# Attention and mixture of experts on one core: the last batch's first loads moved to the head of the second block

## The chip, the cores and the metric

The kernel runs on one core of a Trainium2 chip. The metric is device time in microseconds (us), the median of several executions of the whole program. The core has five engines with a queue of instructions each: TensorE (PE in the rows; PEld is its weight load), VectorE (DVE), ScalarE (ACT), GpSimd (POOL) and SyncE (SP), which issues most of the DMAs.

## The reference, cut to what matters

Kernel-feature attention over 4 batches, 8 heads, 576 positions and head size 64, with 128 features, and then a dense mixture of 4 experts over all 2304 rows, all in fp32:

```python
def phi(x):
    proj = np.einsum('bhsd,md->bhsm', x, omega)
    h = proj - np.sum(x * x, axis=-1, keepdims=True) / 2.0
    h = h - np.max(h, axis=-1, keepdims=True)
    return np.exp(h) / np.sqrt(m)
q_p, k_p = phi(q * scale), phi(k * scale)
kv = np.einsum('bhsm,bhsd->bhmd', k_p, v)
num = np.einsum('bhsm,bhmd->bhsd', q_p, kv)
den = np.einsum('bhsm,bhm->bhs', q_p, k_p.sum(2))[..., None] + 1e-06
x = (num / den)                       # to 2304 rows of 512
for e in range(4):
    out += p[:, e:e + 1] * (np.maximum(x @ w1[e], 0.0) @ w2[e])
```

## The kernel before, in words

The experts' work is cut into visits: one visit is half an expert's hidden units (4 tiles of 128, so 8 visits in all) against one block of rows. The first rows are done in plain visits beside the attention of batches 0 to 2. Then comes the second block, 768 rows, in 8 fast visits (`fast`, L892), and the third block, 1024 rows, in 8 deep ones. Every fp32 operand is split in two parts, a high and a low one (`split`, L562), and every product is three matmuls. A fast visit builds its hidden units from seven products (`product`, L926, `p1` to `p7`) of 6 matmuls for each of two groups. ScalarE's `keep` (L938) copies a product out of PSUM before the next product is added on top of it: the fourth product, `p6(0)`, waits for the copy of the first. After the products come six output tiles of 12 matmuls (`outputs`, L748), and each is added to its accumulator by `gather` (L765), on ScalarE in the first visit of the second block (L780) and on VectorE after that (L782).

Beside its own matmuls a fast visit makes the w1 operands of the next one (`sides`, L672): ScalarE copies the high parts `w1ah` and `w1sh` (L564), GpSimd subtracts for the low parts `w1al` and `w1sl` (L567), VectorE adds in between (`add`, L682). `keep_sides` (L663) writes these operands to DRAM for the third block: eight `kept` stores (L670) per visit. There are two buffers of each kind, so the next visit's `w1ah` cannot be written before this visit's has been stored. The w2 rows come through three `w2r` buffers (L549).

The attention of the last batch has four pairs of heads and is spread over the second block in ticks: `opening` (L375) has six for the first pair (load k; load q; load v and tails; square k; square q; lengths of k), and `later_ticks` (L466) twelve for each pair. A pair needs the projection of keys and of queries on TensorE (`k_ps`, `q_ps`, `t_ps`, L266, L277), maxima and a bias on VectorE (L282 to L293; `nbk`, `nbq` are the biases), exponentials on ScalarE (`kp`, `qp`, L299, L306), squares on GpSimd (L251) with lengths on VectorE (L255), then sums, transposes and quotients.

The order of all work is the order in which the program is written (a manual schedule): each engine and SP's DMA queue run their instructions in that order. `emit` (L1379) runs the visits, and each visit yields after its products and after each output tile; after a yield of 1 the loop takes ticks until their count has reached `done * per`. For the second block `per` is 54 ticks over 44.8 yields.

Of the kernel before, what the change touches and what calls it, by code (L numbers as in the profile page):

```python
# [14 lines left out]
def attention_moe(ctx, tc, kT, qT, kd, qd, kn, qn, vn, omT, probs, w1, w2, out):  # L15
# [11 lines left out]
    _, NP, D, _ = kT.shape  # L27
# [3 lines left out]
    E, FP, P, _ = w1.shape  # L31
# [34 lines left out]
    def bank(name):  # L66
        return psum.tile([P, 512], F32, tag="ps", name=name)
# [33 lines left out]
    NV = len(HALVES)  # L101
# [273 lines left out]
    def opening(p, both=False):  # L375

        p.load("k")
        yield
        p.load("q")
        yield  # L380
        p.load_v()
        p.load_tails()
        yield
        p.square("k")
        yield
        p.square("q")
        yield
        p.lengths("k")
        if both:
            p.lengths("q")  # L390
        yield
# [74 lines left out]
    def later_ticks(pairs):  # L466

        for p, then in zip(pairs, pairs[1:] + [None]):
            p.project("k")
            p.project_tails("k")  # L470
            p.maxima("k")
            p.maxima_tails("k")
            p.bias("k")
            yield
            p.exp_tails("k")
            p.exp("k", 0)
            p.lengths("q")
            yield
            p.exp("k", 1)
            yield  # L480
            p.project("q")
            p.project_tails("q")
            p.maxima("q")
            p.maxima_tails("q")
            p.bias("q")
            yield
            p.exp_tails("q")
            p.exp("q", 0)
            if then:
                then.load("k")  # L490
            yield
            p.exp("q", 1)
            if then:
                then.load("q")
            yield
            p.sum_keys()
            if then:
                then.load_v()
                then.square("k")
            yield  # L500
            p.turn(0)
            yield
            p.turn(1)
            if then:
                then.square("q")
            yield
            p.numerators(0)
            if then:
                then.lengths("k")
            yield  # L510
            p.invert(0)
            p.times(0)
            p.numerators(1)
            yield
            p.invert(1)
            p.times(1)
            yield
# [4 lines left out]
    BIG = {1: (START, 6 * P), 2: (START + 6 * P, 8 * P)}  # L522
# [5 lines left out]
    N0 = len(visits)  # L528
# [204 lines left out]
    def hidden(v, f, n, ps, heads):  # L733
        (a, r), c0 = W[v, "w1", f], visits[v][3]
        for hp in heads:
            w = slice(place(hp) * P, (place(hp) + 1) * P)
            hi, lo = (x[:, c0:c0 + n] for x in x_first[hp])
            nc.tensor.matmul(ps[:, :n], a[:, w], hi, start=(hp == 0), stop=False)  # L738
            nc.tensor.matmul(ps[:, :n], a[:, w], lo, start=False, stop=False)  # L739
            nc.tensor.matmul(ps[:, :n], r[:, w], hi, start=False, stop=(hp == NP - 1))  # L740

    def relu(ps, n):
        ha, hc = (held([P, n], x) for x in ("hh", "hl"))
        nc.scalar.activation(ha, ps[:, :n], AF.Relu)
        nc.vector.scalar_tensor_tensor(hc, ps[:, :n], 0.0, f32(ha), ALU.max, ALU.subtract)
        return ha, hc

    def outputs(v, hs, ps, t, cs):  # L748

        ts_ = slice(t * P, (t + 1) * P)  # L750
        for c in cs:
            (ha, hc), (wa, wc) = hs[c], W[v, "w2", c]
            nc.tensor.matmul(ps, ha[:, ts_], wa, start=(c == 0), stop=False)  # L753
            nc.tensor.matmul(ps, ha[:, ts_], wc, start=False, stop=False)  # L754
            nc.tensor.matmul(ps, hc[:, ts_], wa, start=False, stop=(c == FH - 1))  # L755
# [47 lines left out]
    def plain(v):  # L803
        n = visits[v][4]
        last = v == N0 - 1
        ready = sides(v + 1) if last else iter(())
        hs = []
        for f in range(FH):
            ps = bank("g1")
            hidden(v, f, n, ps, range(2))  # L810
            if n > 2 * P:
                yield 0.5
            hidden(v, f, n, ps, range(2, NP))
            hs.append(relu(ps, n))
            split_w()
            if f != 1:
                next(ready, None)
            if last and f:
                next(building, None)
            yield 0.5  # L820
        tiles = n // P
        for t in range(tiles):
            ps = bank("g2")
            outputs(v, hs, ps, t, range(2))
            if v == N0 - 2 and t in (0, 2):
                next(building)
            if last:
                next(building, None)
            yield 0.5
            outputs(v, hs, ps, t, range(2, FH))  # L830
            gather(v, ps, t)
            gathered(v, t)
            for _ in range(FH // tiles):
                split_w()
            next(ready, None)
            if last:
                next(building, None)
            yield 0.5
# [476 lines left out]
    def first_visit(g1):  # L1315
        hs = [relu(ps, 2 * P) for ps in g1[:2]]
        yield 0.5
        for ps in g1[2:]:
            split_w(lo=nc.vector)
            hs.append(relu(ps, 2 * P))  # L1320
            yield 0.5
        split_w(lo=nc.vector)
        split_w(lo=nc.vector)
        yield 0.5
        for t in range(2):
            ps = bank("g2")
            outputs(0, hs, ps, t, range(FH))
            gather(0, ps, t)
            gathered(0, t)
            split_w()  # L1330
            split_w(lo=nc.vector)
            yield 1
# [40 lines left out]
    def chain(*many):  # L1373
        for x in many:
            yield from x
# [3 lines left out]
    def emit():  # L1379
        pairs, g1 = begin()  # L1380
        later = [Halves(b, hp) for b in range(1, B) for hp in range(NP)]
        windows = {
            0: (first_rest(pairs, opening(later[0], both=True)), 15 / 11),
            3: (joint_ticks(later[:-NP]), 76 / 45.4),
            N0: (chain(opening(later[-NP]), later_ticks(later[-NP:])), 54 / (NV * (BIG[1][1] // P + 1) * 0.8)),
        }
        ticks, n, done, per = iter(()), 0, 0.0, 0
        for v in range(len(visits)):
            if v in windows:
                for _ in ticks:  # L1390
                    pass
                ticks, per = windows[v]
                n, done = 0, 0.0
            for share in first_visit(g1) if v == 0 else fast(v) if v >= N0 else plain(v):
                done += share
                while n < done * per:
                    next(ticks, None)
                    n += 1
        store(0)
# [61 lines left out]
```

## Time and profile before

| | us |
|---|---|
| median of 3 executions | 888.69 (887.83 to 889.95) |
| the profiled execution, its own time | 889.82 |
| its span, first to last instruction | 888.0 |
| second block (8 fast visits) in the span | about 284.5 to 570.7 |
| granted TensorE clock | 1.00 over the span |

The profile shows one execution. Times in its rows are us from the start of the span, durations in the by-line rows are named by their unit. A timeline row merges equal instructions that follow each other ("x4") and ends with the idle time before it and what ended it, where there was any.

### The profile page before, as it was taken

The page shows a single profiled execution, that of the slowest core. Times are in us where ns is not written, and L with a number is a line of the kernel's source. Part 1 is how long each engine was busy: PE and PEld are TensorE (multiplying, and loading weights), DVE is VectorE, ACT ScalarE, POOL GpSimd, SP SyncE. Part 2 cuts the span into 40 slices and gives each one's busy share as a digit, 9 for nine tenths or more (in the row PEclk, how much of TensorE's full clock was granted, in tenths as well). Part 3 has the DMA queues.
Part 4 walks back from the last instruction along what each step waited for, and adds up shares of the span by engine and source line. Part 5 has one row for each costly group of instructions (what it writes and reads, how often), then busy time and mean ns, then how long its engine had stood idle before and what let it go on. Part 6 is the DMA issues. An engine that isn't in the chain of part 4 may idle for free.

```text
span 888.0 us, 14766 instructions
## 1 busy us (share of the span) xinstructions
PE 878.8 (99%) x5484; PEld 789.4 (89%) x5484; DVE 590.9 (67%) x1025; ACT 470.2 (53%) x1039; POOL 563.7 (63%) x494
## 2 busy tenths in 40 slices
PE   9999999999999989999999999999999999999998
PEld 9988888989888888989888899899989898998988
DVE  5765566666677556576766756975858476675847
ACT  6554677776774555555554554544443434444442
POOL 6656465555644454443545346779898887979874
PEclk9999999999999999999999999999999999999999
DMA  7675345444521847536375354644152442415132
GB/s 183 164 223 158 110 161 176 128 137 139 183 72 48 297 123 262 198 131 236 88 262 169 116 213 160 235 152 154 60 178 75 149 155 86 155 60 179 46 121 95
DMA packets 64296, 134.01 MB, mean 151 GB/s; under 512 B 10368, under 2 KB 20800, under 8 KB 64224
## 3 DMA queue, kind: packets, MB, share of 16 engines
q1 hardware_dynamic: 54256, 102.95, 35.3%
q0 software_dynamic: 9360, 29.82, 10.4%
q8 instruction: 43, 0.70, 0.3%
q10 hardware_dynamic: 608, 0.30, 0.1%
q14 instruction: 29, 0.24, 0.1%
HBM read 98.96 MB, written 34.08 MB: 150 GB/s over the span
## 4 chain that ended last, share of the span: by engine, by line
PE 92%; DVE 3%; DMA 2%; issue 1%; POOL 1%; ACT 1%; SPq 0%; POOLq 0%; ACTq 0%
PE g L934 28%; PE g L1009 18%; PE g L753 8%; PE g L755 7%; PE g L754 7%; PE g L738 3%; PE g L739 3%; PE g L740 3%; PE kv L317 2%; PE q_ps L266 1%; PE k_ps L266 1%; PE qt_ps L328 1%; PE k_ps L147 1%; DMA kept<-w1ah 1%; PE q_ps L147 1%
## 5 line engine op out<-in xcount | busy, mean ns | idle before, releaser
L782 DVE SCALAR_TENSOR_TENSOR acc<-g,pr,acc 128x256 f32<-128x256 f32 (+1 forms) x278 | 139.2, 540 | 37.0 <-PE g L755 27.5
L567 POOL TENSOR_TENSOR w2l<-w2r,w2h 128x512 fp32r<-128x512 f32 x61 | 79.3, 1305 | 80.4 <-ACT w2h L564 68.2
L567 POOL TENSOR_TENSOR w1sl<-w1r,w1sh 128x512 fp32r<-128x512 f32 (+1 forms) x43 | 75.1, 1747 | 64.3 <-ACT w1sh L564 53.4
L753 PE MATMUL g<-w2h,hh 128*128 128x512 f32 x280 | 112.0, 400 | 1.8 <-DVE sum L946 1.6
L755 PE MATMUL g<-w2h,hl 128*128 128x512 f32 x280 | 109.7, 392 | 0.0
L754 PE MATMUL g<-w2l,hh 128*128 128x512 f32 x280 | 109.5, 391 | 0.0
L959 DVE SCALAR_TENSOR_TENSOR hl<-sum,hh 128x384 fp32r<-128x384 f32 (+1 forms) x64 | 48.3, 757 | 81.5 <-ACT hh L955 71.7
L946 DVE TENSOR_TENSOR sum<-g,sum 128x384 f32<-128x384 f32 (+1 forms) x96 | 59.3, 619 | 61.2 <-PE g L934 52.8
L934 PE MATMUL g<-xbh,w1sh 128*128 128x384 f32 (+1 forms) x256 | 93.1, 364 | 2.4 <-ACT sum L940 2.4
L934 PE MATMUL g<-xbl,w1sh 128*128 128x384 f32 (+1 forms) x256 | 92.9, 363 | 0.0
L934 PE MATMUL g<-xbh,w1sl 128*128 128x384 f32 (+1 forms) x256 | 92.6, 362 | 0.0
L940 ACT ACTIVATE sum<-g 128x384 f32<-128x384 f32 (+1 forms) x96 | 52.1, 543 | 69.2 <-PE g L934 68.3
L567 POOL TENSOR_TENSOR w1al<-w1r,w1ah 128x512 fp32r<-128x512 f32 (+1 forms) x45 | 51.4, 1157 | 52.2 <-ACT w1ah L564 35.4
L934 PE MATMUL g<-xbh,w1ah 128*128 128x384 f32 (+1 forms) x192 | 70.0, 365 | 0.0
L934 PE MATMUL g<-xbl,w1ah 128*128 128x384 f32 (+1 forms) x192 | 69.6, 362 | 0.0
L934 PE MATMUL g<-xbh,w1al 128*128 128x384 f32 (+1 forms) x192 | 69.5, 362 | 0.0
L753 PEld LDWEIGHTS g<-w2h,hh 128*128 128x128 f32 x280 | 52.6, 188 | 12.7 <-DVE sum L946 2.2
L755 PEld LDWEIGHTS g<-w2h,hl 128*128 128x128 f32 x280 | 52.5, 188 | 11.8 <-DVE hl L992 0.4
L754 PEld LDWEIGHTS g<-w2l,hh 128*128 128x128 f32 x280 | 52.6, 188 | 9.0
L955 ACT ACTIVATE hh<-sum 128x384 fp32r<-128x384 f32 (+1 forms) x64 | 35.0, 548 | 43.9 <-DVE sum L946 43.5
L934 PEld LDWEIGHTS g<-xbh,w1sh 128*128 128x128 f32 x256 | 48.1, 188 | 8.4 <-ACT sum L940 2.7
L934 PEld LDWEIGHTS g<-xbl,w1sh 128*128 128x128 f32 x256 | 48.1, 188 | 5.1
(214 smaller groups left out, 2475.3 us busy)
## 6 DMA issues: line engine op xcount, KB each, us to landing
w1r<-in_w SPq DMA_DIRECT2D x54, 512.0 KB, 3.6
w2r<-in_w SPq DMA_DIRECT2D x76, 256.0 KB, 2.9
kept<-w1sh SPq DMA_DIRECT2D x16, 512.0 KB, 5.0
kept<-w1sl SPq DMA_DIRECT2D x16, 512.0 KB, 5.5
w1sh<-kept POOLq DMA_DIRECT2D x16, 512.0 KB, 4.7
w1sl<-kept POOLq DMA_DIRECT2D x16, 512.0 KB, 5.6
kept<-w1ah SPq DMA_DIRECT2D x16, 384.0 KB, 5.1
kept<-w1al SPq DMA_DIRECT2D x16, 384.0 KB, 5.0
```

Source lines behind the costliest of these rows:

```text
L567: lo.tensor_tensor(c, t, f32(a), ALU.subtract)
L738: nc.tensor.matmul(ps[:, :n], a[:, w], hi, start=(hp == 0), stop=False)
L753: nc.tensor.matmul(ps, ha[:, ts_], wa, start=(c == 0), stop=False)
L754: nc.tensor.matmul(ps, ha[:, ts_], wc, start=False, stop=False)
L755: nc.tensor.matmul(ps, hc[:, ts_], wa, start=False, stop=(c == FH - 1))
L782: nc.vector.scalar_tensor_tensor(to, ps, sc, to, ALU.mult, ALU.add)
L934: nc.tensor.matmul(ps, a[:, w], x[:, k], start=(start and k + at == 0), stop=(k == 1 and at == 2), skip_group_check=not start)
L940: nc.scalar.activation(t, P_[g][where], AF.Copy)
L946: nc.vector.tensor_tensor(t, P_[g][where], t, ALU.add)
L955: nc.scalar.activation(ha, t, AF.Relu)
L959: nc.vector.scalar_tensor_tensor(x, y, 0.0, f32(z), ALU.max, ALU.subtract)
L1009: nc.tensor.matmul(to, x, w, start=(start and f + k == 0), stop=(f + k == 3), skip_group_check=not start)
```

## The change

The three load ticks of `opening` are taken when the second block begins, before its first visit issues anything, and the rate is set to the 51 ticks that are left over the same 44.8 yields.

```diff
-            N0: (chain(opening(later[-NP]), later_ticks(later[-NP:])), 54 / (NV * (BIG[1][1] // P + 1) * 0.8)),
+            N0: (chain(opening(later[-NP]), later_ticks(later[-NP:])), 51 / (NV * (BIG[1][1] // P + 1) * 0.8)),
...
                 ticks, per = windows[v]
                 n, done = 0, 0.0
+                if v == N0:
+                    for _ in range(3):
+                        next(ticks)
```

SP's queue at the start of the second block. Before (the first pair's loads are `k` to `vb`, `kept` are the eight stores of the first visit's operands):

```order
L801 DMA out<-acc 128x512 x2
L549 DMA w2r<-in_w 128x512 x3
L670 DMA kept<-w1ah 128x768
L670 DMA kept<-w1al 128x768
L670 DMA kept<-w1sh 128x1024
L670 DMA kept<-w1sl 128x1024
L670 DMA kept<-w1ah 128x768
L670 DMA kept<-w1al 128x768
L670 DMA kept<-w1sh 128x1024
L670 DMA kept<-w1sl 128x1024
L549 DMA w2r<-in_w 128x512
L247 DMA k<-in_kd 128x576
```

and with the change:

```order
L801 DMA out<-acc 128x512 x2
L247 DMA k<-in_kd 128x576
L247 DMA k<-in_kn 128x576
L247 DMA q<-in_qd 128x576
L247 DMA q<-in_qn 128x576
L128 DMA va<-in_vn 128x4x128
L132 DMA vb<-in_vn 64x4x64
L133 DMA vb<-in_vn 64x4x64
L549 DMA w2r<-in_w 128x512 x3
L670 DMA kept<-w1ah 128x768
```

Seven loads that stood behind three `w2r` loads, eight stores and a fourth `w2r` load now stand in front of them all.

ScalarE's queue at the end of the first visit and the start of the second, whose first `keep` is the row with `sum`. Before:

```order
L564 ACTIVATE w1sh<-w1r 128x1024
L306 ACTIVATE kp<-t_ps,nbk 64x128 x2
L299 ACTIVATE kp<-k_ps,nbk 128x128 x4
L780 ACTIVATE acc<-g_3925,pr 128x512
L299 ACTIVATE kp<-k_ps,nbk 128x128 x4
L940 ACTIVATE sum<-g_3953 128x384
```

and with the change:

```order
L306 ACTIVATE kp<-t_ps,nbk 64x128 x2
L299 ACTIVATE kp<-k_ps,nbk 128x128 x4
L780 ACTIVATE acc<-g_3885,pr 128x512
L299 ACTIVATE kp<-k_ps,nbk 128x128 x4
L780 ACTIVATE acc<-g_3909,pr 128x512
L564 ACTIVATE w1sh<-w1r 128x1024
L780 ACTIVATE acc<-g_3952,pr 128x512
L306 ACTIVATE qp<-t_ps,nbq 64x128 x2
L299 ACTIVATE qp<-q_ps,nbq 128x128 x4
L940 ACTIVATE sum<-g_3986 128x384
```

The exponentials of the keys stood right before that `keep`; now they stand two output tiles earlier, and six exponentials of the queries, which wait for `nbq`, stand in their place.

GpSimd's queue in the first visit. Before:

```order
L567 TENSOR_TENSOR w1al<-w1r,w1ah 128x512
L567 TENSOR_TENSOR w1al<-w1r,w1ah 128x256
L251 TENSOR_TENSOR k<-k 128x576
L567 TENSOR_TENSOR w1sl<-w1r,w1sh 128x1024
L251 TENSOR_TENSOR q<-q 128x576
L567 TENSOR_TENSOR w1sl<-w1r,w1sh 128x1024
```

and with the change:

```order
L251 TENSOR_TENSOR k<-k 128x576
L251 TENSOR_TENSOR q<-q 128x576
L567 TENSOR_TENSOR w1al<-w1r,w1ah 128x512
L567 TENSOR_TENSOR w1al<-w1r,w1ah 128x256
L567 TENSOR_TENSOR w1sl<-w1r,w1sh 128x1024 x2
```

Both squares now stand before the second half of `w1al`, and the two `w1sl` stand together. In the visits behind, the same steps of the four pairs stand one to three output tiles earlier than before, and from the seventh visit on at the same place.

## Rows read from the trace of the kernel before

**Rows 1.** Waits of TensorE, 284 to 576 us: total us, times, longest
```profile
PE g L934 <- ACT sum L940: 2.4, 1, 2.4
PE g L753 <- DVE sum L946: 1.6, 1, 1.6
```
**Rows 2.** Chain that ended last, 300 to 325 us: start, us, what
```profile
307.07 4.84 DMA q<-in_qd
...
316.59 2.33 DVE nbk L293
```
**Rows 3.** Timeline of TensorE, first to second visit: start, us, what
```profile
304.42 0.50 PE L755 MATMUL g<-w2h,hl 128*128 128x512 f32 x1
...
310.31 1.16 PE L266 MATMUL k_ps<-om_r,k 64*128 64x128 f32 x16
...
311.63 0.50 PE L753 MATMUL g<-w2h,hh 128*128 128x512 f32 x1
...
317.20 0.33 PE L934 MATMUL g<-xbh,w1ah 128*128 128x384 f32 x1
...
320.18 0.34 PE L934 MATMUL g<-xbh,w1sl 128*128 128x384 f32 x1
322.89 0.45 PE L934 MATMUL g<-xbh,w1sh 128*128 128x384 f32 x1 [2.37 <-ACT sum L940]
...
338.73 1.16 PE L266 MATMUL q_ps<-om_r,q 64*128 64x128 f32 x16
```
**Rows 4.** Timeline of ScalarE, first to second visit
```profile
299.85 0.94 ACT L564 ACTIVATE w1ah<-w1r 128x512 fp32r<-128x512 f32 x2 [3.00 <-DMA kept<-w1ah]
...
318.95 0.74 ACT L306 ACTIVATE kp<-t_ps,nbk 64x128 f32<-64x128 f32 x2 [2.63 <-DVE nbk L293]
...
320.71 0.70 ACT L780 ACTIVATE acc<-g,pr 128x512 f32<-128x512 f32 x1
321.29 1.17 ACT L299 ACTIVATE kp<-k_ps,nbk 128x128 f32<-128x128 f32 x4
322.29 0.55 ACT L940 ACTIVATE sum<-g 128x384 f32<-128x384 f32 x1
```
**Rows 5.** Timeline of VectorE and of GpSimd, first and second visit
```profile
303.82 0.55 DVE L992 SCALAR_TENSOR_TENSOR hl<-g,hh 128x384 fp32r<-128x384 f32 x1
...
341.96 0.17 DVE L293 SCALAR_TENSOR_TENSOR nbq<-sqq,mxq 128x9 f32<-128x9 f32 x1
...
316.49 2.40 POOL L567 TENSOR_TENSOR w1sl<-w1r,w1sh 128x1024 fp32r<-128x1024 f32 x1
```
**Rows 6.** Timeline of SP's queue, start of the second block
```profile
290.28 0.33 SPq L801 DMA_DIRECT2D out<-acc  x1
...
296.30 0.42 SPq L670 DMA_DIRECT2D kept<-w1ah  x1
```
**Rows 7.** DMA issues, each from a narrow stretch (290.28, 296.30, 479.82, 305.33): KB, us to landing
```profile
out<-acc SPq DMA_DIRECT2D x1, 256.0 KB, 3.9
...
kept<-w1ah SPq DMA_DIRECT2D x1, 384.0 KB, 3.4
...
kept<-w1ah SPq DMA_DIRECT2D x1, 384.0 KB, 5.1
...
k<-in_kd SPq DMA_DIRECT2D x1, 288.0 KB, 4.8
```
**Rows 8.** Stretches of the first visit: us, busy (x) by engine, PEclk, DMA share, GB/s
```profile
290.00:296.00 6.00, 6.00 (x36) 6.00 (x35) 4.63 (x9) 3.64 (x9) 3.27 (x3) 1.00 0.72 255
...
298.00:305.00 7.00, 7.00 (x35) 5.83 (x34) 3.54 (x7) 2.30 (x6) 2.31 (x2) 1.00 1.03 414
305.00:314.00 9.00, 9.00 (x54) 7.30 (x53) 3.86 (x9) 4.38 (x7) 4.06 (x4) 1.00 0.92 301
```
**Rows 9.** Queue q8 in two stretches, 299.6 to 300.4 and 480.2 to 480.6: packets, MB, share
```profile
q8 instruction: 1, 0.02, 7.6%
...
q8 instruction: 1, 0.02, 33.4%
```

## The prediction

> **What bounds the kernel now.** TensorE has no free time to speak of, so I read what makes it wait. The first view is its list of waits over the second block, where the change is: two stand out, 2.4 us once for ScalarE's copy of a product and 1.6 us once for a VectorE sum [rows 1]. The timeline of TensorE says where the first one is: at the start of the second visit the fourth product should begin 0.17 after 320.18, one step of these matmuls, and begins at 322.89, so 2.54 us are lost [rows 3]. The chain of waits, followed back from there, ends in a DMA: the first pair's loads land at 307.07 + 4.84 = 311.91; GpSimd squares them, VectorE makes lengths, maxima and the bias `nbk`, ScalarE, whose queue is in order, waits 2.63 us for that bias, and its copy of the product stands behind the ten exponentials [rows 2, 4]. That is the wait at which the change points. The 1.6 us belong to the sixth visit: there the store of `w1ah` takes 5.1 us to land, where the first visit's takes 3.4 [rows 7]. The change moves nothing there, so I leave it where it is.
>
> The last thing to see is a place without slack. In the first visit ScalarE stands idle 3.00 us until the first `kept` store has landed (296.30 + 3.4 = 299.7) and starts at 299.85 to write the next `w1ah` [rows 4, 6, 7]. The hidden units queue behind it, VectorE's last subtraction runs from 303.82 to 304.37, and the matmul that reads it starts at 304.42 [rows 3, 5]. TensorE waits there already: whatever delays that store delays TensorE by as much.
>
> **What goes: the wait in the second visit.** With the loads in early, the keys' squares, bias and exponentials are through two output tiles sooner. What is late next? ScalarE now has, before its copy, the gather of the sixth output tile, two and four exponentials of the queries, then the copy: 0.58 (320.71 to 321.29) + 0.75 + 1.00 (321.29 to 322.29) + 0.55 = 2.88 us, where 0.75 is the pair's 0.74 and a start [rows 4]. The gather can begin about 0.2 us after the visit does, the copy ends at 3.1, and the fourth product is due at 320.35 - 317.20 = 3.15 [rows 3]. It just fits, if the queries' bias `nbq` is ready 0.8 us into the visit. Their projection is issued one projection and one output tile earlier: 1.32 (310.31 to 311.63) + 2.79 (half of 311.63 to 317.20) = 4.1 us [rows 3]. With VectorE and GpSimd free, bias follows projection by 342.13 - 338.73 = 3.4 us [rows 3, 5], so it would be ready 0.7 us before the visit: 1.5 us to spare. I leave 0.2 us of wait, since ScalarE's sum has no slack: **-2.3 us**. Ends: -2.5 (nothing left) and 0 (another wait of the same size, a rival below).
>
> **What comes: the store in the first visit.** Seven loads now stand between the accumulator's store and the `w2r` loads. By their shapes they are 4 x 288 + 256 + 2 x 64 = 1536 KB; behind them come 3 x 256 KB of `w2r` and the 384 KB of the first `kept` store, 2688 KB or 2.75 MB in all. No earlier run of these loads through this place exists, so I bound it. The accumulator's store lands at 290.28 + 3.9 = 294.2 [rows 6, 7]. From there the DMA engines must carry 2.75 MB. At 414 GB/s, the stretch where the `kept` stores run back to back, that takes 6.6 us: landed at 300.8, or 1.1 us later than today. At 301 GB/s, the stretch in which these seven loads run today, it takes 9.1: 303.3, 3.6 us later [rows 8]. I take each kind at the rate of its own row: 1.57 MB at 301 is 5.2 us, 1.18 MB at 414 is 2.85, landed at 302.3: **+2.6 us**, all of it on TensorE by the chain above. The gap in DMA work that should swallow the loads is too small: between 290 and 296 the engines are busy 0.72 of the time, 1.7 us free [rows 8], against 3.8 us that the loads need even at 414 GB/s.
>
> **What is moved at no cost.** The three `w2r` loads start some 3 us later; the copies that read them stand behind 322.29 in ScalarE's queue, 25 us away. The two squares on GpSimd now stand before the second `w1al`, and VectorE's length of the keys before the first additions: the second visit's `w1sh` operands come up to 2 us later on ScalarE, but GpSimd no longer stands 3 us for a DMA, and TensorE wants them after 319.3. Were that cover gone, every us would be one of TensorE. GpSimd's queue of DMAs is empty in this block. In visits two to six the same steps stand one to three output tiles earlier, with nothing added. Only the fifth visit gets the queries' exponentials right before its first copy, as the second does, and there the gathers are VectorE's, so 0.6 us more is free.
>
> **Sum.** -2.3 + 2.6 = +0.3 us on the profiled execution's own time, 889.82, so 890.1; that execution was 1.1 above the median of the runs, 888.69, so I predict **889.0** for the median. The forecast's own range, from -2.3 + 1.1 to -2.3 + 3.6, is 887.5 to 890.0. About 0.2%, 1.8 us, is what a measurement of this kernel can tell from no change: below 886.9 is faster, above 890.5 slower.
>
> **Rival 1, faster: the store is not held up.** If the loads fill the free DMA time and the store's packets go past what is left of them, the delay is 0 to 0.5 us: 888.69 - 2.3 + 0.2 = 886.6. For it speaks the free time before 296 and that loads read DRAM while the store writes it; against it, that the loads need twice that time. The Trainium skill ("DMA: Bandwidth & Descriptors", section "Two DMAs through the same engine are not ordered") says that descriptors of one queue start in order, though reads and writes are separate queues; by its first half the store waits its turn and this rival falls, and that is what speaks against the change. No run here shows this mix yet. Chance 0.17.
>
> **Rival 2, slower: GpSimd holds the queries' bias.** Today `nbk` takes 2.33 us for 9 columns, from 316.59 to 318.92, just as long as GpSimd's `w1sl` (316.49 + 2.40 = 318.89); with GpSimd idle the same instruction takes 0.17 [rows 2, 5]. With the change that `w1sl` comes behind the gather of the fifth tile and ScalarE's `w1sh`, close to where VectorE reaches `nbq`. If GpSimd starts first, by as little as 0.3 us, the bias comes some 2.4 us into the visit instead of 0.8: 1.6 us of the wait are back, 889.0 + 1.6 = 890.6. The Trainium skill ("SBUF — State Buffer", section "Who interferes with whom") calls the port pair of these two engines an exclusive lock, held for a whole instruction by whichever starts first; the trace agrees, with 2.33 against 0.17. Chance 0.22.
>
> **Rival 3, slower: the store also meets a code fetch.** In the sixth visit a code packet of 0.02 MB (queue q8) runs at 480.4, in the middle of the `w1ah` store, which lands after 5.1 us in place of 3.4 [rows 7, 9]. In the first visit one runs at about 300 [rows 9]: today just behind the first store's landing, with the change in its middle. Another 1.7 us: 890.7. Against it: at 300 the packet's share of the DMA time is small, and the fetch may meet another part of the queue. The Trainium skill ("Runtime: NRT & Kernel Launch", "Instruction fetch mechanics") calls crossing a code page mostly hidden; by that this rival is nothing, but the 5.1 us speak against it. Chance 0.18.
>
> **How the numbers follow.** The forecast keeps 0.43. Below 886.9 lies rival 1 with most of its chance and nothing else: faster 0.17. Above 890.5 lie somewhat more than half of rivals 2 and 3, which can also come together (892.3), and a thin end of the forecast: slower 0.30. Same 0.53. The range for 8 times in 10 goes from 886.8 to 891.3: it takes in rivals 2 and 3 alone and most of rival 1, and leaves out both together.
>
> **What would show it.** Right: SP issues `k` at about 290.8 in place of 305.3; the first `kept` store takes 5 to 7 us to land, ScalarE's `w1ah` starts near 302.5 and TensorE waits 2 to 3 us for VectorE at about 304.3; the wait of 2.4 us for ScalarE's `sum` is gone or under 0.5; the sixth visit's wait is still there. Wrong in term two: the store lands within 3.5 us of issue and before 300.3. Wrong in term one: ScalarE waits for `nbq` at the second visit's start while GpSimd runs `w1sl`. A new wait of TensorE over 0.5 us in visits three to eight would be something that I have not seen.

## The result: 0.65% slower, outside the range

| | before | the change |
|---|---|---|
| median, us | 887.47 (886.50 to 889.95, 6 executions) | 893.48 (891.92 to 895.14, 6 executions) |
| profiled execution, us | 889.82 | 891.92 |
| its span, us | 888.0 | 890.2 |
| granted TensorE clock by execution | 1.000 (profiled) | 1.000 (profiled), 0.998 twice, 0.996 three times |

The ratio is 1.0065 (95% interval 1.0047 to 1.0083), 4.2 to 7.4 us more. 889.0 was forecast, with 886.8 to 891.3 as the range. Two facts stand out before any trace is opened: the profiled executions differ by 2.1 us and the medians by 6.0, and five of the six executions of the change have a mean clock below 1, which the profiled one has not. So one pair of profiles cannot explain the result.

The list of TensorE's waits over the second block, 284 to 576 us, in the changed kernel (us in total, times, longest), to set beside [rows 1]:

```profile
PE g L934 <- ACT sum L940: 5.0, 2, 3.1
PE q_ps L266 <- ACT kp L306: 0.4, 1, 0.4
PE g L753 <- ACT kp L299: 0.2, 1, 0.2
```

The wait has the same name as before, but there are two of it, 3.1 us and 1.9 us, and the sixth visit's 1.6 us for VectorE is not there. The timeline of TensorE says where they are (start, us, what, and in brackets the idle time with its releaser):

```profile
297.59 0.39 PE L755 MATMUL g<-w2h,hl 128*128 128x512 f32 x1
301.11 0.44 PE L934 MATMUL g<-xbh,w1sh 128*128 128x384 f32 x1 [3.14 <-ACT sum L940]
...
428.52 1.04 PE L266 MATMUL q_ps<-om_r,q 64*128 64x128 f32 x13 [0.43 <-ACT kp L306]
...
435.91 0.34 PE L934 MATMUL g<-xbh,w1sl 128*128 128x384 f32 x1
438.10 0.45 PE L934 MATMUL g<-xbh,w1sh 128*128 128x384 f32 x1 [1.85 <-ACT sum L940]
```

What is lost at a place is the distance to the start before it, less the usual step: 301.11 - 297.59 - 0.23 = **3.3 us in the first visit**, where nothing was lost before, and 438.10 - 435.91 - 0.17 = **2.0 us in the fifth**, also new; another 0.7 us is lost at the queries' projection of the fourth visit. The second visit's 2.5 us are gone as forecast. The timeline of ScalarE shows what each of the two stood behind:

```profile
300.05 0.63 ACT L564 ACTIVATE w2h<-w2r 128x512 fp32r<-128x512 f32 x1 [3.48 <-DMA w2r<-in_w]
300.59 0.47 ACT L940 ACTIVATE sum<-g 128x384 f32<-128x384 f32 x1
302.39 0.94 ACT L564 ACTIVATE w1ah<-w1r 128x512 fp32r<-128x512 f32 x2 [1.33 <-DMA kept<-w1ah]
...
435.77 0.74 ACT L306 ACTIVATE qp<-t_ps,nbq 64x128 f32<-64x128 f32 x2 [2.79 <-DVE nbq L293]
436.52 1.14 ACT L299 ACTIVATE qp<-q_ps,nbq 128x128 f32<-128x128 f32 x4
437.54 0.51 ACT L940 ACTIVATE sum<-g 128x384 f32<-128x384 f32 x1
```

In the first visit ScalarE wants the fourth `w2r` tile of this visit, which is the first of the three `w2r` loads behind the moved seven. Those are in SP's queue:

```profile
291.32 0.43 SPq L247 DMA_DIRECT2D k<-in_kd  x1
...
295.28 1.68 SPq L549 DMA_DIRECT2D w2r<-in_w  x3
297.34 0.33 SPq L670 DMA_DIRECT2D kept<-w1ah  x1
```

and their landings, in the list of DMA issues of two narrow stretches at 295.28 and 297.34 (KB, us to landing):

```profile
w2r<-in_w SPq DMA_DIRECT2D x1, 256.0 KB, 4.8
...
kept<-w1ah SPq DMA_DIRECT2D x1, 384.0 KB, 5.0
```

The `w2r` load lands at 295.28 + 4.8 = 300.1. In the kernel before it was issued at 290.76 and took 4.1, 294.9, and its copy ran at 295.85 without a wait (SP's queue, the DMA issues of a narrow stretch at 290.76, ScalarE):

```profile
290.76 5.49 SPq L549 DMA_DIRECT2D w2r<-in_w  x3
...
w2r<-in_w SPq DMA_DIRECT2D x1, 256.0 KB, 4.1
...
295.85 0.62 ACT L564 ACTIVATE w2h<-w2r 128x512 fp32r<-128x512 f32 x1
```

The `kept` store lands at 297.34 + 5.0 = 302.3, where it was forecast. To the tenth that is luck, since the first visit begins 0.6 us later in this profile than in that of before (284.97 against 284.35). Counted from the start of the visit, the `w1ah` that waits for the store comes 1.9 us later than before (2.2 and 1.8 in the two later profiles of the change), not 2.6. Its cost is covered: TensorE is already 3.3 us late.

In the fifth visit the exponentials of the queries stand before ScalarE's `sum` and wait for `nbq`. The timelines of VectorE and then GpSimd there:

```profile
431.75 0.75 DVE L782 SCALAR_TENSOR_TENSOR acc<-g,pr,acc 128x512 f32<-128x512 f32 x1
432.41 1.28 DVE L282 TENSOR_REDUCE mxq<-q_ps 128x4 f32<-128x512 f32 x2
433.60 0.60 DVE L287 TENSOR_REDUCE mxq<-t_ps 64x1 f32<-64x128 f32 x2
434.24 1.23 DVE L292 SCALAR_TENSOR_TENSOR mxq<-sqq,mxq 128x9 f32<-128x9 f32 x1
435.50 0.17 DVE L293 SCALAR_TENSOR_TENSOR nbq<-sqq,mxq 128x9 f32<-128x9 f32 x1
...
433.05 2.39 POOL L567 TENSOR_TENSOR w1sl<-w1r,w1sh 128x1024 fp32r<-128x1024 f32 x1 [5.27 <-ACT w1sh L564]
```

The maxima stand behind an output tile's gather on VectorE, and the two-input `mxq` (1.23 us, alone it takes 0.17) ends just when GpSimd's `w1sl` does, at 435.44. In the kernel before no exponentials stand in front of that `sum`, and it does not wait for `nbq` (ScalarE, VectorE):

```profile
432.21 0.49 ACT L940 ACTIVATE sum<-g 128x384 f32<-128x384 f32 x1 [1.05 <-PE g L934]
...
432.91 0.17 DVE L293 SCALAR_TENSOR_TENSOR nbq<-sqq,mxq 128x9 f32<-128x9 f32 x1
```

From profile to profile: +3.3 - 2.5 + 2.0 + 0.7 - 1.8 (the sixth visit) = +1.7, and 0.6 us of difference were there at 284 us, ahead of everything that was changed. That is the 2.2 us of the spans. What the medians have beyond it had to be found by runs.

### The profile page after: what moved, and what is told of

Its sections match the earlier page's. It is cut to its first block, busy times and chain, and to the rows that moved or that the text cites. A ratio compares the mean times of both kernels' runs of the same rounds, so it can differ in the third digit from the quotient of the medians.

```text
span 890.2 us, 14770 instructions
## 1 busy us (share of the span) xinstructions
PE 878.6 (99%) x5484; PEld 788.5 (89%) x5484; DVE 596.5 (67%) x1025; ACT 469.6 (53%) x1039; POOL 565.0 (63%) x494
## 4 chain that ended last, share of the span: by engine, by line
PE 93%; DVE 4%; DMA 1%; issue 1%; ACT 1%; DVEq 0%; ACTq 0%; SPq 0%
PE g L934 29%; PE g L1009 18%; PE g L753 8%; PE g L755 7%; PE g L754 7%; PE g L738 3%; PE g L739 3%; PE g L740 3%; PE kv L317 2%; PE k_ps L266 1%; PE q_ps L266 1%; PE qt_ps L328 1%; PE k_ps L147 1%; PE kv L177 1%; PE nd L207 1%
```

## The experiments

Each was run beside the kernel before on the same chip, and the ratio is to the kernel before as it ran there; before_third and before_fourth are single executions and have none. "Loads" are the seven that were moved, "steps" the other ticks, which the change puts one to three output tiles earlier.

| run | median us (executions) | before | ratio (95%) |
|---|---|---|---|
| before_again | 885.90 (12) | 887.45 | 0.9987 (0.9973 to 1.0002) |
| after_again | 893.26 (6) | 887.45 | 1.0062 (1.0041 to 1.0084) |
| front_old_ticks | 895.59 (4) | 887.45 | 1.0094 (1.0069 to 1.0119) |
| early_new_ticks | 889.34 (11) | 887.45 | 1.0023 (1.0006 to 1.0040) |
| early_old_ticks | 890.71 (12) | 886.20 | 1.0047 (1.0032 to 1.0061) |
| behind_w2r | 892.67 (5) | 886.20 | 1.0062 (1.0040 to 1.0085) |
| filled | 892.14 (6) | 886.20 | 1.0059 (1.0041 to 1.0077) |
| early_hold | 888.07 (12) | 886.20 | 1.0014 (1.0001 to 1.0027) |
| before_ordered | 886.63 (11) | 886.96 | 0.9996 (0.9983 to 1.0009) |
| soon_old_ticks | 886.06 (12) | 886.96 | 0.9991 (0.9979 to 1.0003) |
| after_third | 894.03 (4) | 886.96 | 1.0079 (1.0063 to 1.0095) |
| filled_again | 893.09 (5) | 886.96 | 1.0070 (1.0055 to 1.0085) |
| front_k | 889.74 (10) | 886.29 | 1.0040 (1.0026 to 1.0055) |
| front_act_queue | 892.60 (4) | 886.29 | 1.0062 (1.0042 to 1.0083) |
| soon_again | 886.81 (12) | 887.08 | 0.9998 (0.9980 to 1.0016) |

### Was the wait that the change removes always there?

The kernel before, profiled three more times. Expected:

> The kernel before, once more, for a second profile of it. Theory: its wait of 2.4 us in the second visit is in every execution, the 1.6 us of the sixth visit (a store that meets a code packet) only in some, since the median of the executions (887.5) is 2.3 below the profiled one (889.8). Then a profile of this run at 887 to 888 shows the first wait and not the second. Rival: both waits are in every execution, and the spread lies elsewhere. TensorE's granted clock is 1.00 by both.

> The kernel before, one more profile. Theory (its wait in the second visit is there only where w1sl starts ahead of nbk): either nbk takes 0.2 us and there is no wait (885 to 887), or it takes 2.3 and there is one of 2.4 (888 to 890); no third way.

> As the run before it. With the two earlier profiles of this kernel (one with the wait, one without) these give four; theory: the wait is in half of them or fewer, so that most executions had nothing there for the change to win.

Measured: 885.95, 887.80 and 890.26 us, and TensorE's wait of 2.4 us in the second visit in none of the three. VectorE's `nbk` and GpSimd's second `w1sl`, from the timelines of before_again:

```profile
315.72 0.17 DVE L293 SCALAR_TENSOR_TENSOR nbk<-sqk,mxk 128x9 f32<-128x9 f32 x1
...
316.38 2.40 POOL L567 TENSOR_TENSOR w1sl<-w1r,w1sh 128x1024 fp32r<-128x1024 f32 x1 [0.72 <-ACT w1sh L564]
```

and of before_fourth:

```profile
316.96 0.17 DVE L293 SCALAR_TENSOR_TENSOR nbk<-sqk,mxk 128x9 f32<-128x9 f32 x1
...
316.99 2.40 POOL L567 TENSOR_TENSOR w1sl<-w1r,w1sh 128x1024 fp32r<-128x1024 f32 x1
```

In the profile that was read for the prediction `w1sl` began at 316.49 and `nbk` at 316.59, and `nbk` took 2.33 us [rows 2, 5]. Here `nbk` begins 0.66 and 0.03 us ahead of `w1sl` and takes 0.17. Which of the two comes first decides 2.5 us, and in this kernel a few hundredths of a microsecond decide which. One profile of four has the wait; in most executions there was nothing here for the change to win. (The Trainium skill, "SBUF — State Buffer", section "Who interferes with whom", says that issue order decides who blocks; the rows agree, 0.17 us for `nbk` where it came first and 2.33 where `w1sl` did.)

So the first half of the theory behind before_again, that this wait is in every execution, fell. The second half, that the sixth visit's wait is only in some, held: it is in before_third (1.7 us) and before_fourth (2.4 us), whose times are therefore above the 885 to 887 expected without the other wait, and absent in before_again. In each of the three profiles with it, a code packet of 16 KB ran at 478.4 to 480.4 us, across the `w1ah` store, which took 5.1 to 6.0 us to land.

Two runs tried to settle that order by hand. In before_ordered GpSimd reads `nbk` before that `w1sl` (cut):

```diff
+            if v == N0 + 1 and i == 1:
+                t = att.tile([P, 1], F32, tag="after_nbk", name="after_nbk", bufs=1)
+                nc.gpsimd.tensor_copy(t, first[0].nbk[:, :1])
             split(tiles[i], sh, sl, nc.scalar, nc.gpsimd)
```

> The kernel before with one small copy added on GpSimd (it reads the keys' bias nbk) in front of the second w1sl of the first visit, so that this w1sl cannot start before nbk is done. Theory (the second visit's wait is decided by which of the two comes first, not by the loads as such): nbk takes 0.2 us and not 2.3 in every execution, no wait of 2.4 us, granted clock 1.00 throughout; 885 to 886, at the low end of the executions of before. Rival (the loads' landing sets it): the wait is there as often as before, 886 to 887.5.

In soon_old_ticks, and once more in soon_again, the loads come right behind the eight `kept` stores, one `w2r` load earlier than before, and the other steps stay (cut; the count of ticks starts at 3):

```diff
         if u == 1:
             keep_sides(v)
+        if v == N0:
+            for _ in range(3):
+                next(ahead[0])
         p4(0)
```

> The kernel before with the seven loads one place further ahead: right behind the eight kept stores, in front of the fourth w2r load. Theory (before loses 2.5 us where the loads land about a microsecond late for nbk to come ahead of w1sl): k lands about 1 us earlier, nbk is done before w1sl begins, no wait in the second visit: 885 to 886.5, clock 1.00. Rival (any earlier landing lets GpSimd's first w1sl run into VectorE's additions, as where the loads came 20 us earlier): the wait stays, 887.5 to 890.

> The loads one place further ahead than before (behind the eight kept stores, in front of the fourth w2r load), once more, since the first comparison (0.9991, 0.9979 to 1.0003) leaves open whether it beats the kernel before. Theory (nbk ahead of w1sl by a microsecond in every execution, and so none of the slower executions of before): 0.5 to 1 us under before, no wait in the second visit. Rival: no difference, as the wait is too rare in before to show in its median.

In all three profiles `nbk` takes 0.17 us and the second visit has no wait, as the theory says; in before_ordered `nbk` still starts at 316.61, and `w1sl` now follows it, at 316.99. In the first profile of before `nbk` began at 316.59, 0.02 us from that, and took 2.33. The medians are 0.3, 0.9 and 0.3 us under before, and every interval includes no difference. That the order alone makes or removes the wait is shown; that it is worth having against the median of before is not. A wait that only a minority of executions have would look like that.

### The loads and the shift of the steps, apart

front_old_ticks has the loads where the change has them and every other step where it was before. early_new_ticks has the steps of the change and the loads in the last plain visit; early_old_ticks has that place for the loads and the old steps, so that on every engine but SP it is the program of before. The first edit is against the change; the second, cut, is common to both early runs, of which early_new_ticks leaves out the change's own three ticks and early_old_ticks starts its count at 3.

```diff
-            N0: (chain(opening(later[-NP]), later_ticks(later[-NP:])), 51 / (NV * (BIG[1][1] // P + 1) * 0.8)),
+            N0: (chain(opening(later[-NP]), later_ticks(later[-NP:])), 54 / (NV * (BIG[1][1] // P + 1) * 0.8)),
...
                     for _ in range(3):
                         next(ticks)
+                    n = 3
```

```diff
+                at += share
+                if v == N0 - 1 and at == 4:
+                    for _ in range(3):
+                        next(windows[N0][0])
```

> The seven loads at the head of the second block as in the change, all other steps where they stood before. Theory (loads and shift of the steps cost apart): the first visit's wait of 3.1 us stays, since the w2r load still lands near 300; the second visit's 2.4 us is gone or under 0.5, since the loads are in 10 us earlier; the fifth visit's 1.9 us is gone, since it comes from the shift: before + 0.9, about 888.5. Rival (the long gap of the first visit brings a lower clock, and that is most of the loss): 890 to 892 with a granted clock under 1.0.

> The seven loads some 20 us earlier, in the middle of the last plain visit, where SP's queue and the DMA engines are idle; all other steps where the change puts them. Theory: w2r and stores land as before, so the first visit's 3.1 us is gone; the second visit's 2.4 us too; the fifth visit's 1.9 us (and 0.7 at its queries' projection) stay: about the time before, 887 to 888.5, at a granted clock of 1.00. Rival (the first visit's wait has another cause than the loads' place in the queue, for example GpSimd's squares in front of w1al): it stays, 890 to 893.

> The seven loads in the middle of the last plain visit, every other step where it stood before: on all engines but SP this is the program of before, word for word. Theory (the loads only had to be out of the way, and the shift of the steps is a cost of its own): the first visit runs as before, the second visit's wait (2.4 us in one profile of before, none in the other) is gone in every execution, no fifth-visit wait: 884 to 886, that is 1.5 to 3 us under before, clock 1.00. Rival (the second visit's wait hangs on the order of nbk and w1sl alone, not on the loads): it turns up in this profile too, and the time is that of before, 886 to 889.

One thing was not as written there: SP issues the early loads at 281.8 to 282.1, not near 267, so they come 9 us earlier than in the change and not 20. (The tiles of `k` and `q` are also the scratch tiles of `build`.)

**early_new_ticks** bore out its theory in the trace: 0.35 us lost where 3.3 were, and 0.6 a little later for VectorE's `hl`; the fifth visit's 2.0 and the fourth's 0.7 are still there. Its median, 889.34, is above the expected 887 to 888.5; six of its 11 executions have a mean clock of 0.998. **front_old_ticks** is the counterpart: 3.8 us lost in the first visit, nothing in the fourth and fifth. So the first visit's loss is the loads' place, but for 1 us at most, and the fourth and fifth visit's is the shift of the steps, by itself enough to make the kernel slower than before.

In one thing **front_old_ticks** and **early_old_ticks** both went against the theory: the wait in the second visit was expected to go and stayed, 2.4 and 2.6 us lost. Both medians are above what theory and rival allowed. In front_old_ticks the rival's lower clock is there as well (0.994 to 0.996 in its four executions), and seven of the 12 executions of early_old_ticks have a mean clock of 0.998 or less. In early_old_ticks the timelines of VectorE and GpSimd show why the wait stayed:

```profile
308.96 1.35 DVE L684 TENSOR_TENSOR w1r<-w1r 128x256 f32<-128x256 f32 x1 [2.19 <-POOL w1al L567]
310.34 2.48 DVE L685 TENSOR_TENSOR w1r<-w1r 128x256 f32<-128x256 f32 x1
312.85 1.25 DVE L686 TENSOR_TENSOR w1r<-w1r 128x256 f32<-128x256 f32 x1
...
316.97 2.31 DVE L292 SCALAR_TENSOR_TENSOR mxk<-sqk,mxk 128x9 f32<-128x9 f32 x1
...
309.99 2.55 POOL L567 TENSOR_TENSOR w1sl<-w1r,w1sh 128x1024 fp32r<-128x1024 f32 x1
...
316.86 2.40 POOL L567 TENSOR_TENSOR w1sl<-w1r,w1sh 128x1024 fp32r<-128x1024 f32 x1 [3.04 <-ACT w1sh L564]
```

and in the kernel before, again VectorE and GpSimd:

```profile
309.05 0.42 DVE L685 TENSOR_TENSOR w1r<-w1r 128x256 f32<-128x256 f32 x1
...
311.92 1.15 POOL L251 TENSOR_TENSOR k<-k 128x576 f32<-128x576 f32 x1 [3.36 <-DMA q<-in_qd]
```

With the loads in early GpSimd does not stand for them at 308.6 to 311.9. It squares at once and starts its first `w1sl` at 309.99, so that its work falls on VectorE's four additions, three of which then take 1.25 to 2.48 us instead of 0.42. VectorE comes to the bias 0.1 us behind the second `w1sl` and is held again. The late loads had kept GpSimd out of VectorE's way. The same program with loads 23 us earlier is 4.5 us slower by the medians.

### What held the w2r load

behind_w2r takes the three load ticks after the first `prepare()` of the first visit, so that only the `w2r` load which this visit needs stands ahead of them. front_k moves the two loads of `k` alone (old steps), and front_act_queue issues all seven from ScalarE's queue (old steps). The edits, cut, are the first against the change and the other two against front_old_ticks.

```diff
         p1(0)
         prepare()
+        if v == N0:
+            for _ in range(3):
+                next(ahead[0])
```

```diff
-                    for _ in range(3):
+                    for _ in range(1):
                         next(ticks)
-                    n = 3
+                    n = 1
```

```diff
-                nc.sync.dma_start(t[:, i], src[which][self.b - 1, self.hp])
+                queue[0].dma_start(t[:, i], src[which][self.b - 1, self.hp])
...
+                    queue[0] = nc.scalar
                     for _ in range(3):
                         next(ticks)
+                    queue[0] = nc.sync
```

> As the change, but the seven loads stand behind the first of the three w2r loads, the one that the first visit itself needs. Theory (that load was what the first visit waited for): no wait for ScalarE's sum near 298; the first kept store still lands near 302 and not 299.7, so a wait of 1.5 to 2.6 us appears near 304, for VectorE's hl behind w1ah; fifth visit's 1.9 us stays: 891 to 893. Rival (the second and third w2r load, or DMA bandwidth as such, held ScalarE): the wait near 298 stays at 3 us, 893 or more.

> Only the two loads of k (576 KB of the 1536) at the head of the second block, all else where it stood before. Theory (bytes ahead in the one queue set when w2r lands): the first w2r lands about 2 us later than before, near 297 in place of 294.8; the wait in the first visit is 0.3 to 1.3 us in place of 3.3; no half clock after it; 887 to 889. Rival (any load ahead of w2r costs the whole wait): 3 us and 890 or more.

> All seven loads at the head of the second block, but issued from ScalarE's DMA queue; all else where it stood before. Theory (order in SP's queue): w2r does not stand behind them and lands within 1 us of before, near 295.5; no wait of 3 us in the first visit; 887 to 889. Rival (the DMA engines' bandwidth, whatever the queue): w2r and the first kept store land 2 us late or more, and TensorE waits 1.5 to 3 us for ScalarE near 298 or for VectorE near 304; 890 or more.

behind_w2r, TensorE's timeline and then ScalarE's:

```profile
304.23 0.40 PE L755 MATMUL g<-w2h,hl 128*128 128x512 f32 x1
307.46 0.50 PE L753 MATMUL g<-w2h,hh 128*128 128x512 f32 x1 [2.84 <-ACT hh L989]
307.80 0.40 PE L754 MATMUL g<-w2l,hh 128*128 128x512 f32 x1
308.64 0.80 PE L755 MATMUL g<-w2h,hl 128*128 128x512 f32 x1 [0.44 <-DVE hl L992]
...
303.33 0.94 ACT L564 ACTIVATE w1ah<-w1r 128x512 fp32r<-128x512 f32 x2 [5.80 <-DMA kept<-w1ah]
```

The wait near 298 is gone, so it was that load's place in the queue, and not the load of the DMA engines as such: the seven loads follow it 0.4 us later. In its place comes the wait that the prediction had put its +2.6 us on, `kept` behind the loads, then `w1ah`, then the hidden units: 3.0 + 0.6 = 3.6 us lost at 307.46 and 308.64, and 3.4 us at half clock behind them. The ratio, 1.0062, is no better than the change's (1.0062 to 1.0079). With the loads at the head of this visit TensorE pays once, for whichever of the two comes first.

front_k lost 0.4 us there (its `w2r`, issued at 291.29, landed after 4.7 us, at 296.0), so how much stands ahead counts: two loads, 576 KB together, cost 0.4 us, and seven, 1536 KB together, cost 3.3. Whether by their bytes or by their number these two runs cannot tell. Its median is above the expected range; in its profile the second visit's 2.4 us were there again, with `nbk` at 316.32 behind a `w1sl` at 316.24, and 3.4 us at half clock after them. In front_act_queue there is no wait near 298, but that does not settle queue against bandwidth, since ScalarE's queue issued the loads from 286.62 on, 4.7 us ahead of the change. Its median, 892.60, is above the expected 887 to 889. The second visit lost 2.4 us here too: of the runs with old steps, all four with the loads more than 10 us early (in front_k those of `k`) have that wait, with VectorE 0.1 us behind `w1sl`. What front_act_queue did show is that another queue is not free. The `w2r` load took 5.5 us to land instead of 4.1 in before, and ScalarE's own timeline has the price of issuing:

```profile
289.63 0.62 ACTq L133 DMA_DIRECT2D vb<-in_vn  x1
290.29 0.49 ACT L942 ACTIVATE sum<-g 128x384 f32<-128x384 f32 x1 [1.88 <-PE g L936]
```

The seven issues take from 286.62 to 290.25 (other work of ScalarE runs beside the first of them), the first `sum` of the visit waits behind the last, and TensorE loses 1.5 us at 290.83.

### The clock after the wait

after_again and after_third are the change once more. filled and filled_again put 18 matmuls of no use where TensorE waits in the first visit (cut):

```diff
         begun(0)
+        if v == N0:
+            g2[1] = bank("g2")
+            for _ in range(18):
+                nc.tensor.matmul(g2[1][:, :n], W[v, "w1", 1][1][0][:, :P], X[1][0][:, 0], start=True, stop=True)
         p7(1)
```

> The changed kernel, once more. Theory: 892 to 895 us; the trace shows again about 3.1 us of wait for ScalarE's sum in the first visit (near 301), behind a w2h copy that waits for its w2r load, and about 1.9 us in the fifth visit (near 438). Five of the six executions have a mean granted clock of 0.996 to 0.998 and are 1.2 to 3.2 us longer than the one at 1.000; if this profile is one of those, it shows a stretch at half clock of some 3.5 to 7 us (0.002 to 0.004 of 890, doubled). Rival: the longer executions have further waits, and the clock is beside the point.

> The change, for comparison with the next run on the same chip: 893, granted clock 0.996 to 0.998 in nearly every execution.

> The change with 18 matmuls of no use put where TensorE waits in the first visit, about 3.1 us of work, into a bank that the next output tile overwrites. Theory (after that wait TensorE runs at half clock for 3.4 us, which costs 1.7 us): the wait shrinks to under 0.7 us, the granted clock of the profile is 1.00 near 303, and the median falls by 1 to 2 us, to 891.5 to 892.3, though nothing of the program got shorter. Rival (the half clock is chance, or comes from something else): the same clock of 0.996 to 0.998 and 893.3 or more.

> The change with 18 matmuls of no use in the place of TensorE's wait in the first visit, beside the change on the same chip. Theory (half clock after the wait): 1 to 2 us under the change, more executions at a clock of 0.999 to 1.000. Rival: the same time within 0.5 us.

Stretches around the wait (us, busy by engine with the number of instructions, PEclk, DMA share, GB/s): after_again,

```profile
296.00:302.70 6.70, 3.26 (x17) 2.65 (x16) 1.17 (x2) 1.57 (x5) 1.73 (x2) 1.00 1.08 395
302.70:306.10 3.40, 3.40 (x10) 2.84 (x10) 1.85 (x2) 1.30 (x3) 2.47 (x3) 0.50 1.03 414
306.10:310.00 3.90, 3.90 (x20) 3.47 (x20) 2.69 (x5) 0.94 (x2) 2.02 (x2) 1.00 0.94 374
```

after_third,

```profile
299.10:305.90 6.80, 6.01 (x17) 5.43 (x18) 1.12 (x2) 2.20 (x5) 5.03 (x5) 0.50 1.03 413
```

and filled:

```profile
296.00:302.70 6.70, 6.55 (x35) 5.79 (x35) 0.65 (x2) 1.61 (x4) 1.28 (x1) 1.00 1.08 388
302.70:306.10 3.40, 3.40 (x19) 3.13 (x19) 2.02 (x3) 1.53 (x5) 2.97 (x3) 1.00 1.03 415
306.10:310.00 3.90, 3.73 (x25) 2.60 (x25) 3.80 (x7) 2.13 (x5) 2.56 (x3) 1.00 0.69 276
```

TensorE stood for 3.0 to 3.4 us in the three profiles of the change. In two of them its granted clock fell to 0.50 (the 1.2 GHz level): in after_again 1.3 us after TensorE had gone on, for 3.4 us, and in after_third while it still stood, for 6.8 us. In the first profile, with the same wait, it stayed at 1.00. In 3.40 us TensorE began 10 matmuls at 0.50 and 19 in the filled run at 1.00, so that stretch cost 3.4 x 9/19 = 1.6 us. The long one cost 2.8: TensorE stood for its first 0.8 us, and the 17 steps from 299.89 took 6.17 us, against 3.42 in the first profile. Filled, the wait shrinks to 0.15 us (at 299.96; 0.26 in filled_again) and the clock stays at 1.00 in both profiles, while the program gets no shorter. Of 16 executions of the change one has a mean clock of 1.000, none 0.999, eight 0.998 and seven 0.996; of 11 executions of the filled one, six are at 0.999 or 1.000 (0.999 comes of a low clock at the very end of the span, as in the profile of filled). By the times alone it would stand open: 893.09 against 894.03 side by side, and the two ratios' intervals overlap; with so few executions the fall of 1 us is no more than likely. Waits elsewhere do it too, but not each time: in front_old_ticks after its first two waits, in before_fourth after the sixth visit's, in behind_w2r after the fifth visit's 2.0 us, but not in the first profile of before after 2.5, nor in early_old_ticks after 2.6.

### The fifth visit

In early_hold the loads are early, the steps as in the change, and one step waits from before the fifth visit to behind its products:

```diff
-                while n < done * per:
+                while n < done * per and not (v == N0 + 3 and at == 6):
```

> The loads in the last plain visit, the other steps as the change puts them, but one step (exponentials of the queries' tails and first half, with the next pair's load of k) waits from before the fifth visit to behind its products. Theory (the fifth visit's 2.0 us comes from those exponentials in front of ScalarE's copy, behind maxima that stand behind VectorE's last gather): that wait is gone, 1.5 to 2 us under the run without the hold (889.3): 887.3 to 888. Rival (VectorE's chain is late whatever stands on ScalarE): a wait of the same size moves a few us back, time unchanged.

Measured: 888.07, ratio 1.0014 against 1.0023 without the hold, and no wait of that size in the trace; 0.4 us are lost a little later, for VectorE's last gather (432.68). The list of TensorE's waits, 284 to 576 us, is

```profile
PE q_ps L266 <- ACT kp L306: 0.4, 1, 0.4
PE g L934 <- DVE acc L782: 0.2, 1, 0.2
PE g L753 <- ACT kp L299: 0.2, 1, 0.2
```

So it was the exponentials' place in front of `sum`. The intervals of the two ratios overlap, so the gain, about 1 us, has its mechanism shown and its size not. VectorE's bias comes even later than without the hold (3.7 us into the visit against 2.7), and it costs nothing, because ScalarE's `sum` no longer stands behind it.

## Why the prediction was wrong

The size and sign follow from the runs. Averages over the three profiles of the change: 3.4 us lost in the first visit (3.3, 3.6 and 3.2), 1.5 by the clock after it (0, 1.6, 2.8), 2.7 in the fourth and fifth: 7.6. Over the four profiles of before: 0.6 in the second visit (2.5 once), 1.6 in the sixth (1.8, 0, 1.9, 2.6), 0.4 by the clock, 0.2 for the load of `k`: 2.8. The difference is 4.8, inside the measured 4.2 to 7.4.

- **The step that failed first**: "The three `w2r` loads start some 3 us later; the copies that read them stand behind 322.29 in ScalarE's queue, 25 us away." This holds for two of the three. The first fills the buffer of the visit's fourth `w2h` copy, at 295.85, 1 us behind its landing. It was costed at nothing and is worth 3.3 us.
- **"What comes: the store in the first visit", +2.6**: the store is held up, by 1.8 to 2.2 us of the visit's own time where the sum says 2.6, and the chain to TensorE is right too: behind_w2r shows it alone (3.6 us there). In the change the `w2r` wait comes first and hides it, so the term is not what TensorE paid. Rival 1 (the store is not held up) is refuted by the store's 5.0 us to landing, against 3.4. Rival 3 did not happen: in the change the code packet ran at 305.0, behind the store.
- **"What goes", -2.3**: in the profiled pair 2.5 us went, and ScalarE's row of exponentials and copy just fitted, as reckoned. It fitted with less slack than that, though: in all three profiles of the change `mxq` took 1.20 us beside GpSimd's `w1sl`, and `nbq` was ready 0.3 us into the visit and not 0.7 before it, where 0.8 was the limit. And the term was read from one execution of a kernel in which the order of two instructions 0.1 us apart decides it. In three profiles of four there was nothing to win.
- **"Only the fifth visit ... there the gathers are VectorE's, so 0.6 us more is free"**: the gather that left ScalarE stands in front of the maxima on VectorE, and the 1.23 us behind `w1sl` come on top. It costs 2.0 us in every profile of the change. This is rival 2's mechanism (GpSimd holds the queries' bias), in another visit than the one named. In the fourth visit, where "nothing added" was written, `w1sl` held the keys' maximum for 1.9 us (425.92; 0.17 in before), and the queries' projection waited for the exponentials behind it: 0.7 us.
- **Not in the sum at all**: that the clock can fall after a wait (1.5 us on average). The forecast knew a granted clock of 1.00 over the whole span and took every microsecond of wait for one microsecond.
- **"I leave it where it is"** for the sixth visit's wait: it is in three of four profiles of before and in none of the three of the change. The kept traces of all runs tell what it hangs on. In the seven profiles in which a code packet runs 0.4 to 1.8 us behind the issue of that visit's first `w1ah` store, the store takes 4.4 to 6.0 us to land and TensorE loses 1.0 to 2.6 us. In the other twelve the packet runs 1.8 us or more ahead of the issue, the store takes 3.3 to 3.5 us, and nothing is lost there. In the change it runs ahead (481.0, the store issued at 483.43). Nothing in the forecast said so: these 1.6 us are luck. The Trainium skill ("Runtime: NRT & Kernel Launch", "Instruction fetch mechanics") calls the cost of crossing a block of code mostly hidden; the store's 4.4 to 6.0 us beside such a packet speak against it here.

## What to carry to other kernels

Before a transfer is moved to the front of a queue, list each transfer it passes with the first instruction that reads it, and not the group's typical one: the one that is due soonest sets the price. A wait that comes from two engines arriving at a shared resource within a tenth of a microsecond is no gain to plan on; profile the kernel several times before you cost its removal. And where an engine was late, ask what it kept out of whose way: here late loads had kept GpSimd clear of VectorE's additions.

## What the runs showed of the hardware

- TensorE's granted clock fell to 0.50 in or just behind waits of 2.0 to 3.8 us, in some executions and not in others of the same program, for 3.4 us (6.8 once). That cost 1.6 us (2.8 once), which makes such a wait up to twice as dear as the idle time in the timeline.
- VectorE's 128x9 instruction with two inputs took 0.17 us when it began 0.03 us ahead of GpSimd's 2.40 us subtraction, and 2.3 us when it began 0.1 us behind it.
- A 384 KB store took 4.4 to 6.0 us to land when a 16 KB code packet ran while it was under way, in seven profiles, and 3.3 to 3.5 us in the twelve in which the packet came ahead of it.
- Seven DMA issues on ScalarE's queue took 3.6 us, 0.35 to 0.62 us each, and held back the work behind them.
